# Attention, a gated mixture and a dense layer in one kernel: where the last layer's table load, w2 residuals, third-block transposes and operand sums are placed

## The chip, the cores and the metric

The kernel runs on one core of one Trainium2 chip. The time is device microseconds (us) of one execution. The engines are TensorE (PE; its weight loads, PEld, run beside its matmuls), VectorE (DVE), ScalarE (ACT), GpSimd (POOL) and SyncE (SP), which issues the DMAs. Each engine works through its own instructions strictly in the order in which the program has them, and waits where an operand or a buffer isn't ready.

## The reference

Three layers follow each other; only the last one changes its schedule here.

```python
x = attention(q, k, v, omega)              # random features, (2304, 512)
P = sinkhorn(x @ w_gate)                   # 8 gates per token, 8 rounds
out = 0
for e in range(8):                         # 8 experts, F = 1024
    out += P[:, e:e+1] * (np.maximum(x @ w1[e], 0.0) @ w2[e])
h = out @ w_in                             # the last layer, F = 2048
g = h * (1.0 / (1.0 + np.exp(-1.702 * h)))
return g @ w_out
```

## The kernel before

The 2304 tokens lie in three blocks j = 0, 1, 2 of 768, each with two halves of 384. Every matrix that enters a matmul is kept as a high part, rounded to the matmul's type, and a residual (`...h`/`...l`), and three matmuls make one product. ScalarE casts the high part, another engine subtracts it for the residual; `split` does both.

Work goes by visits (`visits` in `moe`): one visit is one chunk of 256 hidden columns of one expert for one block. Visits 0 to 19 are expert 0, visits 20 to 103 experts 1 to 7, visits 104 to 127 the last layer, whose chunks are (8, 0) to (8, 7) (`E` is 8), three visits each. A visit has an up part (products into PSUM, then sigmoid or relu and the split of the result, `hh`/`hl`) and a down part (36 matmuls `py`, line 911, added up by `add_up`). Chunk (8, 0) uses the plain up part `up` (48 matmuls `ph`, line 713). All chunks after it use `up_fast` (42 matmuls into `le`, `ri`, `pc`, `pd`, line 822), which needs seven products instead of eight, but wants sums of the block's quarters as operands: `x_sums` makes `th`, `tl` and `x_sum4` overwrites a quarter of `yh`, `yl` with another sum. `up_fast`'s first product goes into `le`, ScalarE copies `le` out to `m` (line 840), and the fourth product adds into the same `le`, so TensorE gets 18 matmuls far before it needs that copy.

The block's new input for the last layer is made by `ffn_in` as a side generator in visits 102, 103 and 104, one block each: TensorE transposes the finished sums `a` into `xt`, ScalarE casts `yh`, VectorE subtracts `yl`. After each of these visits `x_sums` of that block is put into two lanes (`urgent`, one for each kk), after each visit of chunk (8, 0) `x_sum4` of its block; a lane is worked off in order. Line 735 is GpSimd's part of the sums, line 739 VectorE's, lines 762, 771, 772 and 792 are ScalarE's casts.

The order is written out by a planner that runs when the program is built. It has a clock `now`, which advances by the matmuls' estimated time, and a time `pool` until which it believes GpSimd to be busy. After each piece of a visit, `background` takes one step of each lane; a task that comes to `pool_done` gives its step back until the planner's clock has passed GpSimd's time. When `up_fast` is about to be written for a block whose sums aren't written yet, `hurry` writes their steps at once, ahead of the visit, with `force` on, so that nothing gives back.

```python
def pool_busy(us, behind=0.0):
    pool[0] = max(pool[0], now[0] + behind) + us
def until(t):
    while now[0] < t and not force[0]:
        yield
def pool_done():
    return until(pool[0] + 1.0)
# split(r, hi, lo, eng), its last lines:
    if eng is nc.gpsimd:
        pool_busy(0.05 + 0.0023 * r.shape[1] * FC)
# moe, ahead of up_fast:
    while (key, kk) not in sums_done:
        hurry(lane)
```

FC is 256. `split1`, which splits the chunk's first weights on GpSimd, passes views whose shape[1] is 1, 2 or 3 groups of FC elements. `split2` splits `self.r2[:, f, :]`, a view of 128 x 512, so there shape[1] is 512.

Of the kernel before, what the change touches and what calls it, by code (L numbers as in the profile page):

```python
# [10 lines left out]
F32 = mybir.dt.float32  # L11
F32R = mybir.dt.float32r
U32 = mybir.dt.uint32
AF = mybir.ActivationFunctionType
# [6 lines left out]
def tile_performer_sinkhorn_moe(  # L21
# [19 lines left out]
    nc = tc.nc  # L41
# [3 lines left out]
    E, _, F = w1.shape  # L45
    F2 = w_in.shape[1]
    P = 128
# [7 lines left out]
    NF = FC // P  # L55
# [12 lines left out]
    sm = ctx.enter_context(tc.tile_pool(name="sm", bufs=1))  # L68
# [25 lines left out]
    def pool_busy(us, behind=0.0):  # L94
        pool[0] = max(pool[0], now[0] + behind) + us
# [24 lines left out]
    ident = cst.tile([P, P], F32, name="ident")  # L120
# [2 lines left out]
    om_lo = ph["sb"].tile([P, 2 * M], F32R, name="om_lo")  # L123
    wg_raw = ph["sb"].tile([P, NK, E], F32, name="wg_raw")
    wg = ph["sb"].tile([P, NK, 2 * E], F32R, name="wg")
    sm.tile([P, 8], F32, name="pad")
    lg = cst.tile([P, NTILE, E], F32, name="lg")
    pg = lg

# [447 lines left out]
    def split(r, hi, lo, eng):  # L577
        nc.scalar.copy(hi, r)  # L578
        eng.tensor_tensor(out=lo, in0=r, in1=hi.bitcast(F32), op=ALU.subtract)  # L579
        if eng is nc.gpsimd:  # L580
            pool_busy(0.05 + 0.0023 * r.shape[1] * FC)

    class Chunk:
# [58 lines left out]
            i = 0 if o < 3 else 1 if o < 5 else 2  # L642
            return [[x[:, o - self.GROUPS[i][0], kk, :] for x in self.g[i]] for kk in range(2)]

        def split2(self, f):

            pair = [big.tile([P, DM], F32R, tag="w2", bufs=4, name="w2") for _ in "hl"]
            split(self.r2[:, f, :], *pair, nc.vector)
            self.w2.append(pair)

    acc = {}
# [49 lines left out]
    def up(cur, j, halves, prep):  # L701


        h = {}
        run_late()
        for n, (th, f) in enumerate([(th, f ^ th) for th in halves for f in range(NF)]):
            o = ps("ph")[:, :Q]
            m = 0
            for kh in range(2):
                w = cur.quad(cur.SLOT[f, kh])  # L710
                for kk in range(2):
                    for a, x in ((0, blk_h), (1, blk_h), (0, blk_l)):
                        nc.tensor.matmul(  # L713
                            o, w[kk][a], x[j][:, 2 * kh + kk, th * Q : (th + 1) * Q],
                            start=m == 0, stop=m == 3 * NK - 1,
                        )
                        m += 1
            prep(("w2", "", "", "")[n])
            h[th, f] = hi, lo = new_h()
            steps(Act(cur.ch[0], o, hi, lo, sx("g") if cur.ch[0] == E else None))  # L720
            yield 12 * 0.1735
        return h
# [76 lines left out]
    def sum_up(tasks):  # L799
        for lane, t in zip(urgent, tasks):  # L800
            lane.append(t)
# [88 lines left out]
    def down(cur, j, h, halves, first, final):  # L890

        e, _ = cur.ch
        if (e // E, j) not in accs:
            accs.add((e // E, j))
            acc[j] = new_acc(j, "a" if e < E else "o")
        for th in halves:
            outer = cur.fast and e == E and not (final and th == 1 and j == NB - 1)
            py = {}
            halves = range(NF) if th == 0 else range(NF - 1, -1, -1)
            tiles = range(3 * th, 3 * th + 3)  # L900
            if final and th == 1 and j == NB - 1:
                tiles = (5, 3, 4)
            todo = [(f, t) for f in halves for t in tiles] if outer else [(f, t) for t in tiles for f in halves]
            for f, t in todo:
                if t not in py:
                    py[t] = ps("py")
                c = slice(t % 3 * P, (t % 3 + 1) * P)
                hh, hl = h[th, f]
                w2h, w2l = cur.w2[f]
                for m, (a, w) in enumerate(((hh, w2h), (hh, w2l), (hl, w2h))):  # L910
                    nc.tensor.matmul(  # L911
                        py[t], a[:, c], w,
                        start=f == halves[0] and m == 0, stop=f == halves[1] and m == 2,
                    )
                if f == halves[1]:
                    add_up(cur, j, t, py[t], first, final)
                    if t != tiles[0]:
                        run_late()
                yield 3 * 0.2275
# [35 lines left out]
    n_first = len(visits)  # L955
    visits += [((e, c), j, BOTH) for e in range(1, E) for c in range(NCH) for j in range(NB)]
    n_exp = len(visits)
# [32 lines left out]
    def hurry(q):  # L990

        force[0] = True
        run(spare if begun() else q)
        force[0] = False

    def settle(q):
        while q:
            hurry(q)

    may_start = [False]  # L1000
    paused = [False]

    def apply_gate(j):

        for _ in gates:
            pass
        for t in range(ST):
            yield
            o = acc[j][:, t, :]
            nc.scalar.activation(o, o, AF.Copy, scale=pg[:, ST * j + t, 0:1])  # L1010

    def ffn_in(j):

        nblk[j] = hi, lo = new_block("y")
        for g in range(0, ST, 3):
            for t in range(g, g + 3):
                transpose_x(acc[j][:, t, :], t, hi, lo)
            for _ in range(3):
                yield
                if late:  # L1020
                    late.pop(0)()
            for _ in range(3):
                yield
# [3 lines left out]
    def moe():  # L1027

        cn = v = 0
        for idx, (ch, j, halves) in enumerate(visits):  # L1030
            if idx:
                new = ch != visits[idx - 1][0]
                cn, v = (cn + 1, 0) if new else (cn, v + 1)
            cur, nx, n2 = (chunks[cn + i] if cn + i < len(chunks) else None for i in range(3))
            left = 1
            while idx + left < len(visits) and visits[idx + left][0] == ch:
                left += 1
            while idx < n_first and not ready.issuperset((j, th) for th in halves):
                yield None
            may_start[0] = cur.fast and ch[0] < E and left > 1  # L1040
            if idx == n_exp - NB - 1:
                settle(spare)
            if n_exp <= idx < n_exp + NB:
                blk_h[j], blk_l[j] = nblk[j]

            def prep(at, cur=cur, v=v):
                if at == "w2" and v == 0:
                    if cur.fast:
                        cur.split2(len(cur.w2))
                    else:  # L1050
                        cur.split2(0)
                        cur.split2(1)

            key = (ch[0] // E, j)
            side = None
            if n_exp - 2 <= idx <= n_exp:
                side = ffn_in(idx - n_exp + 2)
            elif n_first - 1 <= idx < n_first + 2:
                side = apply_gate(idx - n_first + 1)
            if cur.fast:  # L1060
                for kk, lane in enumerate(urgent):
                    while (key, kk) not in sums_done:
                        hurry(lane)
                todo = up_fast(cur, j, prep)
            else:
                todo = up(cur, j, halves, prep)
            n = 0
            while True:
                try:
                    dt = next(todo)  # L1070
                except StopIteration as end:
                    h = end.value
                    break
                if side and n > 0 and idx >= n_exp - 2:
                    next(side, None)
                n += 1
                yield dt
            if v == 0 and nx:
                nx.load2()
            if nx and left <= 2:  # L1080
                nx.make_sums()
            first = (key, halves[0]) not in seen
            seen.update((key, th) for th in halves)
            paused[0] = left == 1
            for n, dt in enumerate(down(cur, j, h, halves, first, ch == chunks[-1].ch)):
                if n == 2 * len(halves) - 1 and left == 1 and nx:
                    for i in range(3):
                        nx.split1(i, nc.gpsimd)
                    if n2:
                        n2.load1()  # L1090
                    paused[0] = False
                if side and (n > 4 or idx != n_first - 1):
                    next(side, None)
                yield dt
            for _ in side or ():
                pass
            if idx == n_first - 1 or ch == (E, 0):
                sum_up(x_sum4(key, blk_h[j], blk_l[j]))
            if n_exp - 2 <= idx <= n_exp:
                i = idx - n_exp + 2  # L1100
                sum_up(x_sums((1, i), *nblk[i]))
# [71 lines left out]
```

## Time and profile before

| what | value |
|---|---|
| median of 3 runs | 2094.22 us (2094.03 to 2095.5) |
| the profiled execution's own time | 2094.24 us |
| its span | 2092.3 us |
| TensorE busy | 2074.9 us (99%) |
| VectorE, ScalarE, GpSimd busy | 1419.0, 797.1, 501.2 us |
| granted TensorE clock, mean | 0.999 |

The span runs from the first to the last instruction; 1.9 us of the execution's own time lie outside it. A busy TensorE says only that matmuls follow each other; how densely they do is seen from when successive visits begin.

### The profile page before, as it was taken

How to read it: one execution, taken by the hardware profiler on the slowest of the kernel's cores; microseconds unless marked ns; L12 is line 12 of the kernel's file. 1: busy time of each engine (PE TensorE's matmuls, PEld its weight loads, DVE VectorE, ACT ScalarE, POOL GpSimd, SP SyncE). 2: the span in 40 equal slices, each digit the busy share in tenths (PEclk: the TensorE clock that was granted, in tenths of full speed). 3: DMA queues.
4: the chain of work that ended last, by engine and by line, in shares of the span. 5: the costliest groups of instructions: out<-in, count | busy, mean ns of one | idle time of the engine just before them, and what ended most of it. 6: DMA issues, size and time to landing. Idle time of an engine off the chain costs nothing.

```text
span 2092.3 us, 29313 instructions
## 1 busy us (share of the span) xinstructions
PE 2074.9 (99%) x11040; PEld 1883.4 (90%) x11040; DVE 1419.0 (68%) x2630; ACT 797.1 (38%) x1770; POOL 501.2 (24%) x517
## 2 busy tenths in 40 slices
PE   8999999999999999999999999999999999999999
PEld 8999988899899899899998998999989988889988
DVE  7666558876666767667667677675555576676676
ACT  7655543533333223233332232332322355443443
POOL 3222216711221112112211122121111047211110
PEclk9999999999999999999999999999999999999999
DMA  8333211111111111111111111111100000000002
GB/s 163 86 87 92 71 41 61 46 43 46 43 58 54 46 49 50 45 46 43 55 57 43 51 48 46 46 43 29 33 21 21 21 21 21 21 21 21 21 21 91
DMA packets 147966, 100.55 MB, mean 48 GB/s; under 512 B 63600, under 2 KB 125040, under 8 KB 147824
## 3 DMA queue, kind: packets, MB, share of 16 engines
q1 hardware_dynamic: 147824, 98.68, 16.9%
q8 instruction: 87, 1.43, 0.3%
q14 instruction: 55, 0.45, 0.1%
HBM read 85.54 MB, written 13.11 MB: 47 GB/s over the span
## 4 chain that ended last, share of the span: by engine, by line
PE 93%; DVE 4%; ACT 2%; issue 0%; DMA 0%; POOL 0%; SPq 0%; ACTq 0%; DVEq 0%
PE py L911 45%; PE le L822 15%; PE ri L822 10%; PE pc L822 5%; PE pd L822 5%; PE ph L713 5%; PE num L305 2%; PE kv L275 1%; PE xt L343 1%; PE pj L241 1%; PE pj L242 1%; PE pj L243 1%; PE qt L298 1%; PE pt L216 1%; DVE mx L245 0%; ACT feat L261 0%
## 5 line engine op out<-in xcount | busy, mean ns | idle before, releaser
L911 PE MATMUL py<-w,hh 128*128 128x512 f32 x2880 | 895.3, 392 | 2.0 <-DVE hl L684 2.0
L911 PEld LDWEIGHTS py<-w,hh 128*128 128x128 f32 x2880 | 534.7, 188 | 106.2 <-DVE hl L684 2.4
L911 PE MATMUL py<-w,hl 128*128 128x512 f32 x1440 | 564.1, 392 | 2.5 <-DVE hl L684 2.4
L928 DVE SCALAR_TENSOR_TENSOR a<-py,lg,a 128x512 f32<-128x512 f32 x504 | 366.8, 747 | 136.2 <-PE py L911 136.1
L911 PEld LDWEIGHTS py<-w,hl 128*128 128x128 f32 x1440 | 270.5, 188 | 62.0 <-DVE hl L684 4.5
L579 POOL TENSOR_TENSOR g0l<-w,g0h 128x768 fp32r<-128x768 f32 (+1 forms) x52 | 86.9, 1672 | 733.8 <-ACT g0h L578 694.5
L840 ACT COPY m<-le 128x384 f32<-128x384 f32 x105 | 50.5, 481 | 540.2 <-PE le L822 540.2
L563 POOL TENSOR_TENSOR tmp<-tmp 128x256 f32<-128x256 f32 x64 | 47.0, 734 | 629.7 <-DVE tmp L560 331.6
L833 DVE TENSOR_TENSOR pc<-pc,m 128x384 f32<-128x384 f32 x105 | 59.5, 566 | 144.4 <-PE pc L822 140.8
L628 POOL TENSOR_TENSOR w<-w 128x256 f32<-128x256 f32 x140 | 108.4, 794 | 44.6 <-DMA w<-scr_in 22.0
L579 DVE TENSOR_TENSOR w<-r,w 128x512 fp32r<-128x512 f32 x104 | 80.9, 792 | 51.4 <-ACT w L578 51.4
L578 ACT CAST w<-r 128x512 fp32r<-128x512 f32 x104 | 63.7, 629 | 118.6 <-PE py L911 118.2
L686 DVE SCALAR_TENSOR_TENSOR hl<-pc,hh 128x384 fp32r<-128x384 f32 x84 | 46.9, 558 | 84.4 <-ACT hh L678 83.1
L854 ACT COPY u<-le 128x384 f32<-128x384 f32 x105 | 50.4, 480 | 133.5 <-PE le L822 133.5
L261 ACT ACTIVATE feat<-pj,nb 128x128 f32<-128x128 f32 x272 | 74.2, 387 | 68.4 <-DVE nb L257 63.0
L932 DVE TENSOR_TENSOR o<-py,o 128x512 f32<-128x512 f32 x126 | 84.2, 686 | 18.2 <-PE py L911 18.2
L833 DVE TENSOR_TENSOR le<-le,m 128x384 f32<-128x384 f32 x105 | 59.3, 565 | 45.5 <-ACT m L874 45.5
L678 ACT ACTIVATE hh<-ri 128x384 fp32r<-128x384 f32 x84 | 41.4, 493 | 91.8 <-DVE ri L833 91.8
L874 ACT COPY m<-pd 128x384 f32<-128x384 f32 x105 | 50.0, 476 | 55.8 <-PE pd L822 55.8
L822 PE MATMUL le<-th,g2h 128*128 128x384 f32 x210 | 70.2, 334 | 0.3 <-ACT u L854 0.3
L822 PE MATMUL ri<-tl,g0h 128*128 128x384 f32 x210 | 70.4, 335 | 0.0
L822 PE MATMUL ri<-th,g0l 128*128 128x384 f32 x210 | 70.3, 335 | 0.0
(253 smaller groups left out, 4585.9 us busy)
## 6 DMA issues: line engine op xcount, KB each, us to landing
w<-in_moe_w_dram SPq DMA_DIRECT2D x176, 128.0 KB, 2.4
r<-in_moe_w_dram SPq DMA_DIRECT2D x44, 512.0 KB, 3.6
raw<-in_moe_w_in_dram SPq DMA_DIRECT2D x32, 256.0 KB, 3.0
raw<-in_moe_w_out_dram SPq DMA_DIRECT2D x32, 256.0 KB, 2.9
k<-in_k_dram SPq DMA_DIRECT2D x16, 256.0 KB, 4.3
v<-in_v_dram SPq DMA_DIRECT2D x16, 256.0 KB, 4.9
q<-in_q_dram SPq DMA_DIRECT2D x16, 256.0 KB, 4.6
scr_in<-tmp SPq DMA_DIRECT2D x32, 128.0 KB, 1.9
```

The source lines that it names most:

```text
L261: nc.scalar.activation(f[:, h, :], pvs[h // 4][:, h % 4, :], AF.Exp, bias=nb[:, h : h + 1])
L578: nc.scalar.copy(hi, r)
L579: eng.tensor_tensor(out=lo, in0=r, in1=hi.bitcast(F32), op=ALU.subtract)
L628: nc.gpsimd.tensor_tensor(out=r[:, o], in0=r[:, x], in1=r[:, y], op=ALU.subtract)
L713: nc.tensor.matmul(o, w[kk][a], x[j][:, 2 * kh + kk, th * Q : (th + 1) * Q], start=m == 0, stop=m == 3 * NK - 1,)
L822: nc.tensor.matmul(o, a[kk][x], b[kk][y], start=start and kk == 0 and n == 0, stop=kk == 1 and n == 2, skip_group_check=True,)
L833: nc.vector.tensor_tensor(out=o, in0=a, in1=b, op=ALU.add)
L840: nc.scalar.copy(m1, le)
L854: nc.scalar.copy(u2, le)
L911: nc.tensor.matmul(py[t], a[:, c], w, start=f == halves[0] and m == 0, stop=f == halves[1] and m == 2,)
L928: nc.vector.scalar_tensor_tensor(out=o, in0=py, scalar=pg[:, n, e : e + 1], in1=o, op0=ALU.mult, op1=ALU.add)
L932: nc.vector.tensor_tensor(out=o, in0=py, in1=o, op=ALU.add)
```

## The change

Four edits, all for the last layer. In visit 103, between the up and the down part, a sigmoid of one column into an unused tile `pad` makes ScalarE load the sigmoid's table there. For chunk (8, 0) the two w2 residuals are made by GpSimd instead of VectorE. In visit 104 the third block's transposes no longer begin in the up part: the side generator is stepped in the down part alone, from its fourth step on. And in the last layer the lanes are no longer held (`paused`) for the first steps of a chunk's last down part.

```diff
-    sm.tile([P, 8], F32, name="pad")
+    pad = sm.tile([P, 8], F32, name="pad")
...
-        def split2(self, f):
+        def split2(self, f, eng=None):
...
-            split(self.r2[:, f, :], *pair, nc.vector)
+            split(self.r2[:, f, :], *pair, eng or nc.vector)
...
                     if cur.fast:
                         cur.split2(len(cur.w2))
                     else:
-                        cur.split2(0)
-                        cur.split2(1)
+                        for f in range(NF):
+                            cur.split2(f, nc.gpsimd if cur.ch[0] == E else None)
...
-                if side and n > 0 and idx >= n_exp - 2:
+                if side and n > 0 and n_exp - 2 <= idx < n_exp:
                     next(side, None)
...
+            if idx == n_exp - 1:
+                nc.scalar.activation(pad[:, 0:1], ident[:, 0:1], AF.Sigmoid)
...
-            paused[0] = left == 1
+            paused[0] = left == 1 and ch[0] < E
...
-                if side and (n > 4 or idx != n_first - 1):
+                if side and (n > 4 or idx != n_first - 1) and (n > 2 or idx != n_exp):
                     next(side, None)
```

The order of the built programs shows three places. First GpSimd in visits 104 to 106. Before, the sums of block 1 (the rows from the second `u<-yh,t` on) follow straight on, among them `t<-t,yl`, the first step behind `pool_done`:

```order
L735 TENSOR_TENSOR u<-u,yl 128x384
L735 TENSOR_TENSOR u<-yh,t 128x384
L735 TENSOR_TENSOR u<-u,yl 128x384
L735 TENSOR_TENSOR u<-yh,t 128x384
L735 TENSOR_TENSOR u<-u,yl 128x384
L735 TENSOR_TENSOR t<-t,yl 128x384
L735 TENSOR_TENSOR u<-u,yh 128x384
L735 TENSOR_TENSOR u<-u,yl 128x384
```

Now, from the same row on, the two residuals `w<-r,w` stand there, and the last row shown is the last GpSimd row of block 1's sums that is written before chunk (8, 1) is prepared (`L628`, then the splits `g0l`, `g1l`, `g2l`):

```order
L735 TENSOR_TENSOR u<-u,yl 128x384
L579 TENSOR_TENSOR w_16807<-r_16367,w_16806 128x512
L579 TENSOR_TENSOR w_16811<-r_16367,w_16810 128x512
L735 TENSOR_TENSOR u<-yh,t 128x384
L735 TENSOR_TENSOR u<-u,yl 128x384
L735 TENSOR_TENSOR u<-yh,t 128x384
L735 TENSOR_TENSOR u<-u,yl 128x384
L628 TENSOR_TENSOR w<-w 128x256 x4
L579 TENSOR_TENSOR g0l<-w,g0h 128x768
```

Behind those splits twelve rows `L735` now stand without anything between them, the rest of block 1's `x_sums` and block 0's `x_sum4`; before, they were spread over visits 104 to 106 and the following ones.

Second, ScalarE at the start of visit 107 (block 0, the first one with `up_fast` in the last layer). Before, the copies of visit 106's sums are followed by the copy `m<-le` with one cast of w2 ahead of it:

```order
L926 COPY o_17248<-py 128x512 x4
L578 CAST w_17326<-r_16913 128x512
L840 COPY m_17336<-le 128x384
L578 CAST w_17338<-r_16913 128x512
L845 COPY m_17348<-ri 128x384
```

Now eight casts of the sums stand ahead of the copy, the last of them waiting for the last of GpSimd's twelve rows:

```order
L926 COPY o_17209<-py 128x512 x4
L762 CAST th_16791<-u 128x384
L771 CAST th_16791<-t 128x384
L772 CAST th_16791<-u 128x384
L792 CAST yh<-u 128x384
L762 CAST th_16791<-u 128x384
L771 CAST th_16791<-t 128x384
L772 CAST th_16791<-u 128x384
L792 CAST yh<-u 128x384
L578 CAST w_17311<-r_16892 128x512
L840 COPY m_17321<-le 128x384
```

Third, VectorE from the down part of visit 107 to the start of visit 108 (block 1). Before, the steps of the sums stand between the adds `o<-py` of the down part:

```order
L932 TENSOR_TENSOR o_16915<-py,o_16915 128x512 x2
L684 TENSOR_TENSOR hl<-le,hh 128x384
L739 TENSOR_TENSOR tl_17004<-t,th_17003 128x384
L932 TENSOR_TENSOR o_16915<-py,o_16915 128x512
L739 TENSOR_TENSOR tl_17004<-u,th_17003 128x384
L932 TENSOR_TENSOR o_16915<-py,o_16915 128x512
L739 TENSOR_TENSOR yl<-u,yh 128x384
L932 TENSOR_TENSOR o_16915<-py,o_16915 128x512 x2
```

Now all six adds come first, then ten rows of the sums of block 2 and of block 1's fourth sum, both lanes one behind the other, and only then visit 108's first own add `pc<-pc,m`:

```order
L932 TENSOR_TENSOR o_16894<-py,o_16894 128x512 x2
L684 TENSOR_TENSOR hl<-le,hh 128x384
L932 TENSOR_TENSOR o_16894<-py,o_16894 128x512 x4
L739 TENSOR_TENSOR t<-yh,t 128x384
L739 TENSOR_TENSOR tl_16995<-u,th_16994 128x384
L739 TENSOR_TENSOR tl_16995<-t,th_16994 128x384
L739 TENSOR_TENSOR tl_16995<-u,th_16994 128x384
L739 TENSOR_TENSOR yl<-u,yh 128x384
L739 TENSOR_TENSOR t<-yh,t 128x384
```

On TensorE only the two groups of transposes `xt` of visit 104 move: the first from the up part, behind the second `ph`, to behind the fourth step of the down part, the second to behind its tenth step. SyncE's DMAs keep their order.

## Rows read from the trace of the kernel before

**Rows 1.** The page: span, and engines with busy us, share and instructions.

```profile
span 2092.3 us, 29313 instructions
PE 2074.9 (99%) x11040; PEld 1883.4 (90%) x11040; DVE 1419.0 (68%) x2630; ACT 797.1 (38%) x1770; POOL 501.2 (24%) x517
```

**Rows 2.** Waits of TensorE, whole span: us in total, times, longest.

```profile
PE py L911 <- DVE hl L684: 4.4, 4, 2.0
```

**Rows 3.** Timeline of TensorE: first matmuls of visits 104 to 110; start, us.

```profile
1701.19 0.33 PE L713 MATMUL ph<-yh,g0h 128*128 128x384 f32 x1
...
1724.31 0.33 PE L713 MATMUL ph<-yh,g0h 128*128 128x384 f32 x1
...
1740.86 0.33 PE L713 MATMUL ph<-yh,g0h 128*128 128x384 f32 x1
...
1757.40 0.33 PE L822 MATMUL le<-yh,g0h 128*128 128x384 f32 x1
...
1774.62 0.33 PE L822 MATMUL le<-yh,g0h 128*128 128x384 f32 x1
...
1792.81 0.34 PE L822 MATMUL le<-yh,g0h 128*128 128x384 f32 x1
...
1808.33 0.33 PE L822 MATMUL le<-yh,g0h 128*128 128x384 f32 x1
```

**Rows 4.** Timeline of TensorE in visit 104; idle before and releaser in brackets.

```profile
1705.39 1.47 PE L343 MATMUL xt<-ident,a 128*128 128x128 f32 x12
...
1714.43 1.22 PE L911 MATMUL py<-w,hh 128*128 128x512 f32 x2 [2.02 <-DVE hl L684]
```

**Rows 5.** Windows in visit 104: us, busy of PE, PEld, DVE, ACT, POOL, PEclk, DMA.

```profile
1714.50:1717.50 3.00, 3.00 (x8) 2.34 (x9) 2.45 (x6) 1.08 (x3) 0.00 (x0) 0.50 0.00 0
1717.50:1718.00 0.50, 0.50 (x5) 0.50 (x4) 0.50 (x1) 0.48 (x1) 0.00 (x0) 0.62 0.00 0
```

**Rows 6.** Timelines of ScalarE and VectorE in visit 104.

```profile
1703.54 1.28 ACT L668 ACT_TABLE_LOAD   x1 [1.75 <-PE ph L713]
1704.84 0.50 ACT L668 ACTIVATE g<-ph 128x384 f32<-128x384 f32 x1
...
1704.32 2.36 DVE L579 TENSOR_TENSOR w<-r,w 128x512 fp32r<-128x512 f32 x2
```

**Rows 7.** Timelines of GpSimd, ScalarE and TensorE at visit 107's start.

```profile
1756.94 1.29 POOL L579 TENSOR_TENSOR g2l<-w,g2h 128x512 fp32r<-128x512 f32 x1
...
1757.60 0.59 ACT L926 COPY o<-py 128x512 f32<-128x512 f32 x1 [0.77 <-PE py L911]
...
1758.72 0.48 ACT L840 COPY m<-le 128x384 f32<-128x384 f32 x1
...
1760.55 0.33 PE L822 MATMUL le<-th,g1h 128*128 128x384 f32 x1
```

**Rows 8.** Windows, line 735 alone, 1690 to 1800: us, GpSimd busy (count).

```profile
1690.00:1800.00 110.00, 49.78 (x44) 0.98 0.06 20
```

**Rows 9.** Line 735, whole span: count, ns min/median/max, first and last start.

```profile
L735 POOL TENSOR_TENSOR u<-u,yl x18: 1006/1122/1357, 1685.9 to 1782.5; 128x384 f32<-128x384 f32 x18
```

**Rows 10.** Groups by form, 1690 to 1800: count, busy us, mean ns, idle before.

```profile
L739 DVE TENSOR_TENSOR tl<-u,th 128x384 fp32r<-128x384 f32 x12 | 11.6, 971 | 2.0 <-ACT th L762 2.0
...
L579 DVE TENSOR_TENSOR w<-r,w 128x512 fp32r<-128x512 f32 x4 | 4.8, 1228 | 2.9 <-ACT w L578 2.9
...
L792 ACT CAST yh<-u 128x384 fp32r<-128x384 f32 x6 | 3.1, 514 | 4.8 <-POOL u L735 4.8
...
L578 ACT CAST w<-r 128x512 fp32r<-128x512 f32 x4 | 2.5, 624 | 3.6 <-PE py L911 3.5
```

**Rows 11.** Timeline of VectorE: one residual of the sums, one add.

```profile
1745.33 0.55 DVE L739 TENSOR_TENSOR yl<-u,yh 128x384 fp32r<-128x384 f32 x1
...
1776.04 0.68 DVE L932 TENSOR_TENSOR o<-py,o 128x512 f32<-128x512 f32 x1
```

## The prediction

> **What bounds the kernel now.** I read the page first: TensorE is busy for 2074.9 of 2092.3 us [rows 1], so the kernel can gain only where TensorE stands or runs slowly. Then the waits of TensorE: the largest entry is `py` waiting for VectorE's `hl`, 4.4 us in four pieces [rows 2], line 684, which is used by the last layer alone. The third view is the timeline at the first matmul of successive visits [rows 3]. From 1792.81 to 1808.33 a visit with `up_fast` takes 15.52 us; that is the pace at which nothing is in the way. Visit 107 (from 1757.40) takes 17.22 us, 1.70 too much, visit 108 (from 1774.62) 18.19 us, 2.67 too much. Visit 105 (from 1724.31), with the plain up part, takes 16.55 us; visit 104 takes 23.12 us, and of its surplus two groups of transposes of 1.47 us [rows 4] are work, so at most 16.55 + 2.94 = 19.5 us are due and 3.6 us are lost.
>
> These 3.6 us have two parts. TensorE stands for 2.02 us until VectorE has written `hl` [rows 4], and when it starts again its granted clock is 0.50, the lower level of 1.2 GHz: for 3.00 us in full and for a part of the next half microsecond, whose mean is 0.62 [rows 5], so (1 - 0.62) / 0.5 x 0.5 = 0.4 us more. 3.4 us at half rate cost 1.7 us. Both together, 3.7 us, are the loss. In all, the stretch from visit 104 to 108 holds 3.6 + 1.7 + 2.7 = 8.0 us that a better order could give back.
>
> **The change, part by part.** *Table load.* It takes 1.28 us on ScalarE, and the first sigmoid follows at once, at 1704.84 [rows 6]. In visit 104 it is the first link of the chain sigmoid, multiply, cast, residual that TensorE's down part waits for; removed, that chain starts 1.3 us earlier. In visit 103 it stands ahead of three casts `yh` and the splits of the next weights, and the down part's 36 matmuls cover it; I cost it at nothing there, and at 1.3 us if that cover were gone. The Trainium skill (ScalarE: Activation LUTs, section What ACT_TABLE_LOAD costs) counts about 1380 ns of draining besides the load, 2.66 us in all; this trace shows no second part behind the load, and by the figure of the Trainium skill the chain in visit 104 would start 1.4 us earlier still, which leaves the sum as it is.
>
> *Residuals of w2.* Two subtractions leave VectorE, 2.36 us [rows 6], directly ahead of the first multiply. They end at 1706.68, while the first sigmoid was ready at 1705.34, so they hold the chain up by 1.34 us. With the load's 1.28 us that is 2.62 us, more than the 2.02 us for which TensorE stands. On GpSimd the same size takes 1.29 us [rows 7], 2.6 us for both; there they stand behind the last `u<-u,yl` of block 0 and are wanted only when the down part begins, 48 matmuls into the visit, about 8 us.
>
> *Transposes.* They are the same 24, later; what they wait for and release moves into the down part, where the bound below keeps half the old loss. I take the whole surplus of visit 104 as removed: -3.6 us.
>
> *What the residuals do to the planner.* This is the part on which the sum rests. `split` books GpSimd with 0.05 + 0.0023 x shape[1] x 256. For the 768 wide split that is 1.8 us, for w2's view, whose shape[1] is 512, it is 301.5 us, twice: the planner believes GpSimd busy for 603 us, longer than all that is left. Every task of the sums that comes to `pool_done` now gives its step back until it is forced. So the sums of blocks 1 and 2 and all fourth sums aren't written in the background of visits 104 to 106 any more, but at once, ahead of visits 107 and 108, as the three places of the order show. The fourth edit (no pause) changes nothing then: what would run on is parked anyway.
>
> *Visit 107.* Times from its first matmul. TensorE gets as far as the first matmul into `le` that needs the copy `m<-le`: 1760.55 - 1757.40 = 3.15 us [rows 7]. ScalarE has that copy behind eight casts, and these follow GpSimd's twelve adds. GpSimd comes to the first add when the split `g2l` is done, 1756.94 + 1.29 = 1758.23, that is 0.83 us. An add takes 49.78 / 44 = 1.13 us in this stretch [rows 8], twelve 13.6 us. Once in the first lane GpSimd waits for ScalarE's cast and VectorE's `tl`, as `u` is overwritten: the last copy `o<-py` ends 0.79 us into the visit [rows 7], a cast of 0.51 and a `tl` of 0.97 us [rows 10] end at 2.3, the add before them at 2.0: 0.3 us. Between the lanes it waits for the cast `yh`, 0.51 us [rows 10], VectorE's `yl` and then `t`, 0.55 us each while GpSimd is idle [rows 11]: 1.6 us. At the end come the cast `yh`, the cast of w2, 0.62 us [rows 10], and the copy itself, 0.48 us [rows 7]: 1.6 us. Sum 0.83 + 13.6 + 0.3 + 1.6 + 1.6 = 17.9 us, less 3.15 us: TensorE waits 14.8 us. Then it does 12 matmuls in 2.1 us (4.2 us at the lower clock) up to the product that needs the copy `u<-le`. That copy is behind the sigmoid of `pc`, and `pc` behind two residuals of w2, 1.23 us each [rows 10], and two `t` of about 0.6 us on VectorE; with the add, sigmoid and copy at some 0.5 us each that is 5.2 us, of which 0.5 us were the copy `m<-le`: 4.7 us after the start. So 2.6 us are lost here, be it as a wait or as slow clock. Visit 107 takes 15.5 + 17.4 = 32.9 us: +15.7.
>
> *Visit 108.* Here VectorE holds the sums back: `t<-yh,t` stands behind the six adds of visit 107's down part, the last of which ends about 0.9 us into the visit (the last matmul's end and 0.68 us [rows 11]). Then `t` 0.55, twelve adds 13.6, 1.6 between the lanes, `yh` 0.51 and the copy 0.48 make 17.6 us, less 3.15: a wait of 14.5 us. No w2 is split here, so the clock counts: I put it at the same 1.7 us as in visit 104. 15.5 + 16.2 = 31.7 us: +13.5. The six adds of visit 109's fourth sum need nothing that is late, and GpSimd does them while TensorE works on visit 108.
>
> **Sum.** -3.6 + 15.7 + 13.5 = +25.6 us. The profiled execution took 2094.24 us (2092.3 of span and 1.9 outside), the median of the runs shown is 2094.22, so one base serves both: **2119.8 us**, 1.2% slower.
>
> **Bounds.** An add lies between 1.006 and 1.357 us [rows 9]: over 24 adds -3.0 or +5.4 us. The second loss in visit 107 may be nothing (-2.6), the clock may hold in visit 108 (-1.7), or stay low twice as long after waits seven times as long as the one seen (+1.7 there, +2 in visit 107). Visit 104 may keep half its loss (+1.8). That spans 2112.5 to 2130.7. I take the middle rows, since the adds in the hurried chain run beside VectorE's subtractions as those in rows 8 do. On GpSimd the Trainium skill (GPSIMD Engine Reference, section 3.1 Elementwise, side-by-side cycle accounting) gives 2.6 cycles at 1.2 GHz for an element of a two-input operation; for 384 elements that is an estimate of 0.83 us, where the row has 1.13, and by it the sum would be 24 x 0.3 = 7.2 us less, 2112.6.
>
> **Rivals.** (1) *Faster*: the forced sums hide, because the chain is done before `m<-le` is due; then only the 8.0 us are given back, 2086.2. It decides at 3.15 us into visit 107: the copy would have to end by then, and before the change it does, starting 1.32 us into the visit [rows 7]. Against it: twelve adds of 1.13 us in front of it in GpSimd's and ScalarE's order. 5 in 100, 4 of them faster and 1 within the bound when half is given back. (2) *Only visit 107 waits*: GpSimd works ahead on visit 108's sums while 107 stands, 2119.8 - 16.2 = 2103.6. For it: four of their adds are written earlier. Against: VectorE's order puts `t<-yh,t` behind the adds of the down part. 7 in 100. (3) *Visit 109 waits too*: its six adds begin only at its first matmul: 0.8 + 6.8 + 1.0 - 3.15 = 5.4 us, 2125.2. 6 in 100. (4) *Everything at the low bounds*: VectorE mostly waits in the forced chain, GpSimd's adds run at their shortest, and neither clock nor second loss counts: 2112.5. Against: `tl` and the adds still run side by side. 5 in 100.
>
> **Chances.** The forecast has 77 in 100, with 2113 to 2127 as its own range. 2110 to 2130 leaves out rivals 1 and 2 (12) and the forecast's far ends (about 7). A change of this kernel can be told from none at about 0.2%, 4.2 us: faster 0.04, within 0.01, slower 0.95.
>
> **What would show it.** In the profile after: TensorE's waits led by `le` waiting for ScalarE's `m` at line 840, twice, 14 to 15 us; visits 107 and 108 of 32 to 33 us, 104 of about 19.5 and no `hl` wait in it; a granted clock of 0.50 behind each long wait; GpSimd with 12 adds in a row there and ScalarE idle with `yh` waiting for `u`; the table load in visit 103 and TensorE not waiting for it. The prediction is wrong if the copy `m<-le` isn't late, if the waits are much shorter than twelve adds, or if visit 104 still stands for `hl`.

## The result and the profile after

The changed kernel takes 2120.9 us in the median (2119.79 to 2122.09), the kernel before, run beside it, 2094.86 us: ratio 1.0122, 95% interval 1.011 to 1.0134. 2119.8 us was predicted. The profiled execution took 2119.79 us, with a span of 2117.9 us: 25.6 us more span than before [rows 1].

The page after shows that TensorE is hardly busier, 2075.3 us where it had 2074.9; nearly all the added time is standing time. In the busy tenths (40 slices of some 53 us) it is one slice of TensorE that drops to 5:

```profile
span 2117.9 us, 29314 instructions
PE 2075.3 (98%) x11040; PEld 1885.0 (89%) x11040; DVE 1414.7 (67%) x2628; ACT 797.5 (38%) x1771; POOL 502.2 (24%) x519
...
PE   8999999999999999999999999999999995999999
```

The waits of TensorE over the whole span have a new first line (in total, times, longest), and `hl`, which led before [rows 2], has all but gone:

```profile
PE le L822 <- ACT m L840: 28.5, 2, 14.3
...
PE py L911 <- DVE hl L684: 0.3, 1, 0.3
```

TensorE's timeline, the first matmuls of visits 104 to 110 as in [rows 3], with the waits among them in brackets:

```profile
1701.20 0.33 PE L713 MATMUL ph<-yh,g0h 128*128 128x384 f32 x1
...
1714.18 0.74 PE L911 MATMUL py<-w,hh 128*128 128x512 f32 x2 [0.40 <-ACT o L926]
...
1721.15 0.34 PE L713 MATMUL ph<-yh,g0h 128*128 128x384 f32 x1
...
1737.70 0.33 PE L713 MATMUL ph<-yh,g0h 128*128 128x384 f32 x1
...
1754.24 0.33 PE L822 MATMUL le<-yh,g0h 128*128 128x384 f32 x1
...
1771.71 0.69 PE L822 MATMUL le<-th,g1h 128*128 128x384 f32 x1 [14.15 <-ACT m L840]
...
1786.61 0.33 PE L822 MATMUL le<-yh,g0h 128*128 128x384 f32 x1
...
1804.24 0.69 PE L822 MATMUL le<-th,g1h 128*128 128x384 f32 x1 [14.31 <-ACT m L840]
...
1818.19 0.33 PE L822 MATMUL le<-yh,g0h 128*128 128x384 f32 x1
...
1833.72 0.33 PE L822 MATMUL le<-yh,g0h 128*128 128x384 f32 x1
```

Differences of neighbouring rows: visit 104 takes 19.95 us (before 23.12), 105 and 106 are unchanged at 16.55 and 16.54, 107 takes 32.37 (17.22), 108 takes 31.58 (18.19), and 109 has 15.53 us, the undisturbed pace. -3.17 + 15.15 + 13.39 = +25.37 of the 25.6 us.

What stands behind the long wait in visit 107 is seen on GpSimd (timeline, first from the last splits on) and on ScalarE:

```profile
1750.40 1.84 POOL L579 TENSOR_TENSOR g0l<-w,g0h 128x768 fp32r<-128x768 f32 x1 [28.07 <-PE py L911]
1752.20 1.29 POOL L579 TENSOR_TENSOR g1l<-w,g1h 128x512 fp32r<-128x512 f32 x1
...
1754.70 1.01 POOL L735 TENSOR_TENSOR t<-t,yl 128x384 f32<-128x384 f32 x1
1756.21 1.01 POOL L735 TENSOR_TENSOR u<-u,yh 128x384 f32<-128x384 f32 x1 [0.50 <-DVE tl L739]
1757.29 1.19 POOL L735 TENSOR_TENSOR u<-u,yl 128x384 f32<-128x384 f32 x1
1758.44 0.99 POOL L735 TENSOR_TENSOR u<-yh,th 128x384 f32<-128x384 f32 x1
...
1763.45 1.24 POOL L735 TENSOR_TENSOR t<-t,yl 128x384 f32<-128x384 f32 x1 [1.68 <-DVE t L739]
...
1769.23 0.99 POOL L735 TENSOR_TENSOR u<-u,yl 128x384 f32<-128x384 f32 x1
1772.55 1.25 POOL L735 TENSOR_TENSOR u<-yh,t 128x384 f32<-128x384 f32 x1 [2.33 <-DVE t L739]
```

```profile
1693.57 1.28 ACT L1083 ACT_TABLE_LOAD   x1
1694.87 0.20 ACT L1083 ACTIVATE pad<-ident 128x1 f32<-128x1 f32 x1
...
1770.25 0.51 ACT L792 CAST yh<-u 128x384 fp32r<-128x384 f32 x1 [2.79 <-POOL u L735]
1770.67 0.61 ACT L578 CAST w<-r 128x512 fp32r<-128x512 f32 x1
1771.19 0.47 ACT L840 COPY m<-le 128x384 f32<-128x384 f32 x1
...
1775.31 0.47 ACT L854 COPY u<-le 128x384 f32<-128x384 f32 x1
```

Twelve adds, the first at 1754.70, the last ending at 1770.22, then the cast `yh`, a cast of w2 and the copy `m<-le`, whose end at 1771.66 lets TensorE go on at 1771.71. Before, that copy started 1.32 us into the visit [rows 7]; now 16.95 us. GpSimd itself had been idle for 28.07 us ahead of `g0l`, which waited for TensorE, and the adds stand behind `g0l` in its order: it was not short of time, its work had been written late.

In each of the two waits the granted clock falls, and TensorE runs on at the lower clock, 0.50, behind it (windows: us, busy time of PE, PEld, DVE, ACT, POOL, granted clock, DMA share, GB/s):

```profile
1770.00:1775.00 5.00, 3.29 (x10) 3.29 (x11) 4.03 (x6) 2.38 (x6) 2.59 (x3) 0.50 0.00 0
1775.00:1780.00 5.00, 5.00 (x22) 4.30 (x22) 3.30 (x7) 2.91 (x7) 2.21 (x3) 0.83 0.34 107
...
1804.00:1807.00 3.00, 2.76 (x9) 2.76 (x10) 1.68 (x3) 1.44 (x5) 2.84 (x4) 0.50 0.00 0
1807.00:1810.00 3.00, 3.00 (x18) 3.00 (x17) 1.86 (x4) 1.11 (x4) 2.84 (x4) 0.93 0.00 0
```

### The profile page after: what moved, and what is told of

The parts are those of the page before. It is cut to its first block, busy times and chain, and to the rows that moved or that the text cites. A ratio compares the mean times of both kernels' runs of the same rounds, so it can differ in the third digit from the quotient of the medians.

```text
span 2117.9 us, 29314 instructions
## 1 busy us (share of the span) xinstructions
PE 2075.3 (98%) x11040; PEld 1885.0 (89%) x11040; DVE 1414.7 (67%) x2628; ACT 797.5 (38%) x1771; POOL 502.2 (24%) x519
## 4 chain that ended last, share of the span: by engine, by line
PE 94%; DVE 3%; ACT 1%; POOL 1%; issue 0%; DMA 0%; SPq 0%; ACTq 0%; DVEq 0%
PE py L911 45%; PE le L822 16%; PE ri L822 10%; PE pd L822 5%; PE pc L822 5%; PE ph L713 5%; PE kv L275 2%; PE num L305 2%; POOL u L735 1%; PE pj L241 1%; PE pt L216 1%; PE pj L242 1%; PE pj L243 1%; PE qt L298 1%; PE xt L343 1%; ACT feat L261 0%
## 5 line engine op out<-in xcount | busy, mean ns | idle before, releaser
L628 POOL TENSOR_TENSOR w<-w 128x256 f32<-128x256 f32 x140 | 108.3, 794 | 45.6 <-DMA w<-scr_in 22.7
L822 PE MATMUL le<-th,g1h 128*128 128x384 f32 x210 | 71.0, 338 | 28.5 <-ACT m L840 28.5
L822 PE MATMUL le<-th,g1l 128*128 128x384 f32 x210 | 71.1, 339 | 0.0
L822 PE MATMUL le<-tl,g1h 128*128 128x384 f32 x210 | 71.1, 339 | 0.0
```

The lines of the kernel that those rows point to most:

```text
L628: nc.gpsimd.tensor_tensor(out=r[:, o], in0=r[:, x], in1=r[:, y], op=ALU.subtract)
L822: nc.tensor.matmul(o, a[kk][x], b[kk][y], start=start and kk == 0 and n == 0, stop=kk == 1 and n == 2, skip_group_check=True,)
```

## The experiments

Three theories were to be told apart. B: the booking of 603 us alone makes the planner hold the sums back until they are forced. G: GpSimd's 2.6 us of new work delays them. P: the fourth edit, the sums that no longer pause, puts them in the way. The table has all kernels; the visits' lengths are differences of their first matmuls in each trace, as above. Each ratio is to the executions of before that were run beside that kernel: their median is 2094.86 us for the change, 2095.37 for e1 to e4, 2095.4 for e5 to e8 and 2095.28 for e9.

| kernel | visit 104 | 107 | 108 | median us | ratio to before, 95% |
|---|---|---|---|---|---|
| before | 23.12 | 17.22 | 18.19 | 2094.86 | |
| the change | 19.95 | 32.37 | 31.58 | 2120.9 | 1.0122 (1.011 to 1.0134) |
| e1 all four edits, booked right | 19.85 | 19.31 | 16.83 | 2093.13 | 0.9989 (0.9979 to 0.9999) |
| e2 the booking alone | 22.66 | 32.01 | 32.46 | 2123.63 | 1.0134 (1.0119 to 1.0149) |
| e3 edits 1, 3, 4 | 21.53 | 20.10 | 17.21 | 2094.85 | 0.9999 (0.9989 to 1.0008) |
| e4 edit 2 alone | 21.43 | 32.38 | 31.57 | 2121.36 | 1.0123 (1.0108 to 1.0138) |
| e5 e1 and `hl` in its visit | 19.90 | 16.87 | 17.09 | 2090.69 | 0.9978 (0.9969 to 0.9987) |
| e6 edit 2, booked right | 21.43 | 17.21 | 18.18 | 2092.93 | 0.9991 (0.9982 to 1.0) |
| e7 edits 1 and 3 | 21.50 | 17.22 | 18.21 | 2094.09 | 0.9993 (0.9985 to 1.0002) |
| e8 edits 1 to 3, booked right | 19.85 | 17.19 | 18.20 | 2090.89 | 0.9981 (0.9972 to 0.999) |
| e9 e8 and e5's line | 19.87 | 16.32 | 18.07 | 2091.05 | 0.9979 (0.997 to 0.9988) |

**e1**, the changed kernel with one line of `split` mended:

```diff
-            pool_busy(0.05 + 0.0023 * r.shape[1] * FC)
+            pool_busy(0.05 + 0.0023 * (r.shape[1] * FC if len(r.shape) > 2 else r.shape[1]))
```

> The whole change, but `split` books GpSimd with the size of the 2-dimensional view (512 elements, 1.2 us) where it booked 301.5 us. Theory B (the booking alone makes the planner hold the sums back until they are forced): no wait of 14 us on `le`, the losses of visits 104, 107 and 108 mostly gone; the record of the kernel before shows 8.0 us that can be recovered there, so 2087 to 2091 us, faster than the kernel before. Theory G (the 2.4 to 2.6 us of subtractions on GpSimd really delay the sums): the two waits stay, 2118 to 2122 us. Theory P (the sums that no longer pause get in the way): the same 2118 to 2122 us.

Measured: 2093.13 us, no wait of 14 us. G and P fall: the same subtractions run on GpSimd and the sums don't pause, and yet 27.8 us are gone. But it missed B's own 2087 to 2091 us. Visit 104 is as good as it should be (19.85), and visit 107 has become worse, 19.31 us. Its two waits on TensorE's timeline:

```profile
1760.69 0.44 PE L822 MATMUL le<-th,g2h 128*128 128x384 f32 x1 [1.06 <-ACT u L854]
...
1771.81 0.50 PE L911 MATMUL py<-w,hl 128*128 128x512 f32 x1 [2.15 <-DVE hl L684]
```

The larger one is explained by VectorE's order of e1 ahead of that `hl`:

```profile
1766.96 0.55 DVE L672 TENSOR_TENSOR le<-le,g 128x384 f32<-128x384 f32 x1
1767.43 0.90 DVE L739 TENSOR_TENSOR tl<-u,th 128x384 fp32r<-128x384 f32 x1
1768.48 1.15 DVE L739 TENSOR_TENSOR tl<-t,th 128x384 fp32r<-128x384 f32 x1
1769.55 0.54 DVE L739 TENSOR_TENSOR tl<-u,th 128x384 fp32r<-128x384 f32 x1
1770.02 1.27 DVE L932 TENSOR_TENSOR o<-py,o 128x512 f32<-128x512 f32 x2
1771.22 0.54 DVE L684 TENSOR_TENSOR hl<-le,hh 128x384 fp32r<-128x384 f32 x1
```

Three `tl` and two adds stand ahead of `hl<-le,hh`, whose cast `hh` ScalarE had ended at 1768.03. Counted in order from block 0's sums on, these `tl` belong to block 2's; they stand there because each lane is worked off in order and has them ahead of block 1's fourth sum, which visit 108 needs.

**e2**, the kernel before with the planner's clock of GpSimd set forward, and no instruction added or moved by hand:

```diff
                         cur.split2(0)
                         cur.split2(1)
+                        if cur.ch[0] == E:
+                            pool_busy(603.1)
```

> The kernel before with nothing added but 603.1 us on the planner's clock of GpSimd behind the last chunk's split of w2; the subtractions stay on VectorE and no instruction is new. Theory B: the waits on `le` of 14 to 15 us appear in visits 107 and 108 (+15.7 and +13.5 us by the prediction, and what visits 107 and 108 lose now is in that), and visit 104 keeps its 3.6 us: 2094.9 + 25.6 + 3.6 = about 2124 us, 2120 to 2126. Theories G and P: nothing was moved to GpSimd and the pause is there, so 2093 to 2096 us.

Measured: 2123.63 us, 28.3 more than the 2095.37 us of before beside it, and the same line in TensorE's waits:

```profile
PE le L822 <- ACT m L840: 28.4, 2, 14.3
```

A number in the planner is enough to bring the whole loss. B is shown.

**e3** undoes the second edit in the changed kernel (`prep` calls `cur.split2(0)` and `cur.split2(1)` on VectorE again).

> The change without its second edit: both residuals of w2 stay on VectorE; the table load in expert 7, the later transposes and the sums without their pause are as in the changed kernel. Theories B and G: no wait of 14 us, a part of the 8.0 us given back; the residuals still stand ahead of the first multiply with 2.36 us, so some of visit 104's loss may stay: 2088 to 2093 us. Theory P: the waits stay, 2118 to 2122 us.

Measured: 2094.85 us, as before. P falls a second time; the gain expected beside it did not come either. Visit 104 keeps 1.53 us of waiting, for ScalarE's copy `o<-py`, and visit 107 stands 2.15 us for `hl` as in e1.

**e4**, the kernel before with the second edit alone, booked at 301.5 us each:

```diff
-                        cur.split2(0)
-                        cur.split2(1)
+                        for f in range(NF):
+                            cur.split2(f, nc.gpsimd if cur.ch[0] == E else None)
```

> The kernel before with the second edit alone: both residuals of w2 on GpSimd, booked with 301.5 us each; the table load, the transposes and the pause are as before. Theories B and G: the two waits of 14 to 15 us, and visit 104 better by the 1.3 us that the residuals hold up its chain: 2094.9 + 15.7 + 13.5 - 1.3 to -3.6 = 2120 to 2123 us. Theory P: the pause stands, so no long wait, 2090 to 2095 us.

Measured: 2121.36 us, with visits 107 and 108 as in the changed kernel to 0.01 us. The other three edits change nothing there, as the prediction had it for the pause.

**e5**, e1 with the last residual of a visit written beside the others:

```diff
-        if e == E:
+        if e == E and cur.ch != (E, 1):
             late.append(a4.last)
         else:
             a4.last()
```

> The whole change with the right booking (as e1), and one line more: in the last chunk the fourth activation writes its residual `hl` in the up part, behind its own cast, instead of in the down part behind the sums' `tl` and two adds into `o`. In the trace of e1 visit 107's `hl` starts at 1771.22 us although its cast `hh` had ended at 1768.03, and TensorE waits 2.15 us for it; in visit 108 0.87 us. Theory Q (what is left of the gain is lost to VectorE's order): these two waits go, at most 0.5 to 1.5 us of others come in their place, so 1.5 to 3 us less than e1: 2090 to 2092 us, ratio to before 0.9975 to 0.9985. Theory V (VectorE has too much work there in any order): another wait of the same size, 2092.5 to 2094.5 us.

Measured: 2090.69 us, theory Q. VectorE's timeline of e5 has `hl` ahead of the sums, and among TensorE's waits of the stretch 1690 to 1900 no `hl` is left:

```profile
1767.13 0.55 DVE L672 TENSOR_TENSOR le<-le,g 128x384 f32<-128x384 f32 x1
1768.23 0.56 DVE L684 TENSOR_TENSOR hl<-le,hh 128x384 fp32r<-128x384 f32 x1 [0.55 <-ACT hh L676]
1768.70 0.89 DVE L739 TENSOR_TENSOR tl<-u,th 128x384 fp32r<-128x384 f32 x1
```

```profile
PE le L822 <- ACT u L854: 1.9, 2, 1.1
PE py L911 <- ACT o L926: 0.3, 1, 0.3
```

**e6** is e4 with e1's line in `split`.

> The kernel before with the second edit alone, and booked with 1.2 us each. Theory B: the two waits of 14 us are gone, so 26 us less than e4; visit 104 lacks the residuals' 1.34 us in its chain and keeps the table load: its 3.6 us of loss become about 1 to 2.3 us; 2092 to 2095 us. If GpSimd's subtractions cost by themselves what the booking says they delay: above 2096 us.

Measured: 2092.93 us, 28.4 us less than e4 (0.9991 against 1.0123 of before). Visit 104 gains 1.69 us, visits 107 and 108 are as before.

**e7** has only the first and the third edit (the lines on `pad`, and the two conditions on `side`).

> The kernel before with the first and the third edit alone: the table load in expert 7 and the later transposes; the residuals of w2 stay on VectorE and the sums pause. With e3 (the same and no pause) it gives the price of the pause. If the pause is worth nothing here (as the prediction has it): the time of e3 within 0.1%, 2093 to 2096 us. If the sums that don't pause cost visit 107 its time: 1 to 2.5 us less than e3.

Measured: 2094.09 us; visit 104 gains 1.62 us. Against e3, visits 107 and 108 together are 35.43 instead of 37.31 us, so running on without the pause costs something in these traces, the lower clock behind e3's wait of 2.15 us included (below). The 1.88 us overstate it: e3's trace is of an execution above its median (2095.81 us), e7's of one below (2092.71). The medians differ by 0.76 us, less than their intervals, and do not decide it.

**e8** is e1 with `paused[0] = left == 1` as before.

> The whole change with the right booking, but with the pause kept (the fourth edit undone). If the fourth edit is worth nothing: the time of e1 within 0.1%, 2092 to 2094 us. If running on brings the sums ahead: 1 to 2 us more than e1 and a longer loss in visit 107. If it is the sums' `tl` of visit 108 that hold `hl` up because they come earlier: 1 to 2 us less.

Measured: 2090.89 us. The third case holds in direction: visits 107 and 108 take 35.39 us against 36.14 in e1. That is 0.75 us by the traces; the medians show 2.2 us, but the two intervals overlap, so I hold to the smaller figure. The times bear it out: where an execution's mean granted clock is 1.000, e1 takes 2091.48 to 2091.6 us (four executions) and e8 2090.62 to 2091.01 (seven).

**e9**, e8 with e5's line.

> e8 (the whole change, right booking, pause kept) with e5's line as well: the fourth activation of the last chunk writes `hl` in the up part. If the two gains add: e8 loses 0.77 and 1.46 us in front of `hl` in visits 107 and 108 by its trace; without them 1 to 2.2 us less than e8, 2088.7 to 2090 us, and faster than e5. If the pause only moves the sums behind `hl` into the start of visit 108 (VectorE has the same work before `m<-le` is due): a wait on `le` or `u` of 1 to 2 us in visit 108 instead, and the time of e5 and e8, 2090 to 2091.5 us.

Measured: 2091.05 us; the gains do not add. The wait has moved to the start of visit 108, as the second case said (TensorE's timeline):

```profile
1776.70 0.44 PE L822 MATMUL le<-th,g1h 128*128 128x384 f32 x1 [1.56 <-ACT m L840]
```

e5, e8 and e9 all beat both kernels, the one before by about 0.2%, and cannot be told apart by their medians. At a mean granted clock of 1.000 e5 takes 2089.39 to 2089.51 us and e9 2089.54 to 2089.96, both below e8's 2090.62 to 2091.01: the line on `hl` is worth about 1 us with the pause too, but brings no second gain on top of e5. What e5 still loses, 1.06 us in visit 107 and 0.88 in visit 108 in front of the `le` that needs `u`, was left as it is, and no run shows what would give it back.

## Why the prediction was right, point by point

*The planner.* That the booking parks the sums was the step on which all rested, and it had the formula and the order of the instructions behind it, but no row of the trace. e2 shows that it suffices, e1 and e6 that without it the loss is gone.

*Visit 104*: -3.6 predicted, -3.17 measured. The wait for `hl` is gone from it; what was not foreseen is 0.40 us of waiting for ScalarE's copy `o<-py`. The table load cost nothing in visit 103, as said: that visit takes 18.16 us (first matmuls at 1683.04 and 1701.20) where it took 18.15 (1683.04 and 1701.19). e6 (-1.69) and e7 (-1.62) give half each; together, e8 has -3.27.

*Visit 107*: a wait of 14.8 us predicted, 14.15 measured. The first add came 0.46 instead of 0.83 us into the visit, and the twelve adds took 12.98 us (6.38 and 6.60 a lane) instead of 13.6, 1.08 us each; the gaps were 0.50 and 1.68 us (0.3 and 1.6 predicted). Another 0.36 us lie between the other adds, which the prediction had at nothing, and the end with the two casts and the copy took 1.44 us (1.6). The copy was done 17.42 us into the visit (17.9), and TensorE had reached it after 3.32 us (3.15). The second loss was 32.37 - 15.53 - 14.15 = 2.69 us (2.6 predicted, as a wait or as slow clock). In the trace slow matmuls fill that time: the twelve behind the wait take 4.12 us, from 1771.71 to 1775.83, and no wait is shown in front of the `le<-th,g2h` that needs `u`. But the copy `u` ended only at 1775.78, 0.05 us before that matmul, and what it had waited for was VectorE, so at the full clock TensorE would have stood there for it; the trace does not say how much of the loss the clock adds.

*Visit 108*: a wait of 14.5 us predicted, 14.31 measured; the clock's loss is 31.58 - 15.53 - 14.31 = 1.74 us (1.7). It begins as foreseen: `t<-yh,t` comes 0.81 us into the visit, behind the adds of visit 107's down part. There the copy `u` waits for TensorE (0.98 us), so this loss is the clock's. *Visit 109* does not wait: rival 3 falls, as rivals 1 and 2 do by the two waits.

So the largest error was the length of an add, 1.09 us on average over the 24, where 1.13 was taken; the low bound of 1.006 us came from one group of the adds, and others took 0.99. The errors of visits 104 and 107 offset each other (-3.17 for -3.6, +15.15 for +15.7): that the sum fits better than its parts is luck. The Trainium skill (GPSIMD Engine Reference, section 3.1 Elementwise, side-by-side cycle accounting) gives the 2.6 cycles from which the estimate of 0.83 us came. The trace agrees with that as a slope: 768 columns take 1.84 and 384 take 0.99 us, 2.2 ns a column or 2.66 cycles at the 1.2 GHz that the Trainium skill gives there. What the estimate lacked is a fixed part, by these two rows an estimate of 0.99 - 0.85 = 0.14 us, and what GpSimd loses beside VectorE: the five of visit 107's twelve adds that began while a VectorE subtraction was running took 1.19 to 1.24 us, the other seven 0.99 to 1.01.

*One step failed without touching the number*: that all 8.0 us of visits 104, 107 and 108 could come back, on which rival 1's 2086.2 us rested. e8, free of the booking's fault, gets back visit 104's share, and keeps 17.19 + 18.20 us in the other two, 4.3 us more than twice 15.53. That loss has a cause of its own. VectorE's order ahead of `hl` is shown to hold a part of it: e9, which differs from e8 in that line alone, has 1.0 us less in the two visits, and e5, without the pause, 1.4. What the rest, some 3 us, comes from stays open.

## What to carry to other kernels

Where a scheduler books costs, a moved operation is also a new entry in its books: work out what the cost formula says for the new operand's shape before costing the instruction itself. A dimension read from the wrong place cost 28 us here (28.4 between e4 and e6, 27.8 between the change and e1), where the moved work takes 2.6. And a low share of busy time does not make an engine's work free: GpSimd, busy for 24% of the span, was idle for 28 us and then held TensorE up for 14, because its work had been written late.

## What was not expected of the hardware

*The same instruction on VectorE takes 0.69 or 1.49 us*, with what GpSimd does meanwhile (VectorE's timeline of the changed kernel):

```profile
1756.29 1.34 DVE L739 TENSOR_TENSOR tl<-t,th 128x384 fp32r<-128x384 f32 x1 [0.16 <-ACT th L771]
...
1771.31 0.69 DVE L579 TENSOR_TENSOR w<-r,w 128x512 fp32r<-128x512 f32 x1
...
1772.86 1.49 DVE L579 TENSOR_TENSOR w<-r,w 128x512 fp32r<-128x512 f32 x1
```

GpSimd is idle during the first `w<-r,w`; when the second begins, GpSimd's add runs already, from 1772.55 to 1773.80, and 1773.80 plus the 0.69 us of the first gives 1774.49, where 1774.35 is measured. The `tl` in the first row, 0.55 us alone, began in the same way while GpSimd's add of 1756.21 to 1757.22 ran: 1757.22 + 0.55 = 1757.77, where 1757.63 is measured. That is as if whichever began second stood until the first was nearly through. The Trainium skill (SBUF — State Buffer, section Who interferes with whom) says just this of a VectorE instruction with two inputs in SBUF beside a GpSimd instruction that reads SBUF; these rows agree.

*A wait of the same length did not always bring the lower clock.* e1 and e3 both stand 2.15 us for `hl` in visit 107. Behind it the clock stays at 1.00 in e1, the first line, and falls to 0.50 in e3, the last two:

```profile
1771.50:1775.00 3.50, 3.19 (x16) 2.89 (x17) 3.50 (x7) 0.67 (x2) 3.34 (x4) 1.00 0.02 5
```

```profile
1774.50:1775.50 1.00, 0.98 (x4) 0.83 (x5) 1.00 (x2) 0.00 (x0) 0.92 (x2) 0.89 0.00 0
1775.50:1778.50 3.00, 3.00 (x10) 2.61 (x9) 2.57 (x5) 0.51 (x1) 2.84 (x4) 0.50 0.02 5
```

e3's visits 107 and 108 are together 1.17 us longer than e1's. In both traces the wait comes 11.12 us behind the same wait for `u`, so its length and its place do not decide it; and executions of one kernel differ too, the ten of e1 with mean granted clocks of 0.998 to 1.000 and times of 2091.48 to 2096.42 us. What decides is open. The two waits of 14 us and that of 2.02 us before the change [rows 4, 5] were all followed by 0.50.
